# Splitting the product p4 and adding the residual by accumulating DMA in the channel stage of a hash-attention and mixer kernel

## Chip, cores, metric

One core of a Trainium2 chip. The metric is the device time of one execution in microseconds. "Span" is the length of the profiled execution, some 1.8 us shorter than its device time.

## The reference, cut to what matters

```python
# attention (hash-masked), then a mixer on x of shape (4, 768, 512):
h = np.maximum(xt @ w_tok1, 0.0) @ w_tok2
u = x + h.transpose(0, 2, 1)
h2 = np.maximum(u @ w_ch1, 0.0) @ w_ch2     # d_ch = 1536
return u + h2                               # u is the residual
```

The change touches only the last two lines: the channel stage.

## The kernel before

The channel stage is f32. It runs over three blocks (`s`) of 1024 rows. Each of the two matrix products is done by the Strassen-Winograd scheme: seven block products instead of eight. In the second product five of the seven are split once more (`product`, 21 matmuls of 256 columns) and two are done whole (`whole_product`, 12 matmuls of 512 columns): p1 and p4. The first product, with its relu, is done in six "hidden" steps a block. In the kernel's terms, products lie in PSUM tiles and everything else on the chip in SBUF tiles; an "eviction" reads a product from PSUM.

```python
def product(s, j, name, q, between):
    ...
    part(0, 4, b00)                                                  # TensorE
    part(1, 5, b10)
    p1 = copy(ps[0], "p1", ...)                                      # ScalarE
    nc.vector.tensor_tensor(b00, b11, b01, op=ALU.subtract)          # operand sums
    part(2, 0, b01)
    part(3, 1, extra())
    nc.vector.tensor_tensor(b10, b10, b00, op=ALU.subtract)
    ...
    for work in between:
        work()                                                       # adds that combine products
    ...                                                              # evictions into q
    if j + 1 < 6:
        begin(ORDER[j + 1])                                          # two sums for the next product
    ...

def outputs(s):
    ...
    product(s, 3, "p3", q3, [add(q57, q7, q5), residual(q57, 1, 1), residual(q7, 1, 0)])
    product(s, 4, "p6", q6, [add(q3, q3, q5), residual(q3, 0, 1)])
    product(s, 5, "p2", q2, [
        add(q6, q6, q1), add(q57, q57, q6), store(q57, 1, 1), add(q3, q3, q6), store(q3, 0, 1),
        add(q7, q7, q6), residual(q1, 0, 0),
    ])
    ps = whole_product(s, 6, "p4")
    add(q2, q2, q1)()
    store(q2, 0, 0)()
    ...                                       # sums for the next block; last adds and stores of q7
```

`residual` is a VectorE add of the kept `XT`, `store` a plain DMA from SyncE. The hidden steps of each block carry extra work on VectorE: in block 0 the jobs that prepare the split weights (`parts`, through one buffer `seen`), later `look()`, which loads 768 KB of q and k into that same single buffer and reduces it to a maximum; the 16 looks check that the fast softmax is safe.

```python
def look():
    if seen:
        t, n = seen.pop(0)
        nc.vector.tensor_reduce(largest[:, n : n + 1], t, AX.XY, ALU.max, apply_absolute_value=True)
    if unseen:
        n = unseen.pop(0)
        t = pool.tile([P, 2, S], F32, name="seen", tag="seen", bufs=1)
        nc.sync.dma_start(out=t, in_=qk[pairs[n][0], pairs[n][1]])
        seen.append((t, n))
```

And one line of the host code that turns out to matter, though no DMA of this kernel comes from GpSimd:

```python
nc = bacc.Bacc("TRN2", target_bir_lowering=False, num_devices=1, dynamic_dma_scratch_size=1024)
```

I read it as the room, 1024 bytes in each SBUF partition, for the descriptors (the entries that tell the DMA engines what to move) of DMAs that GpSimd issues.

## Time and profile before

| | before |
|---|---|
| device time, median (range) | 827.37 us (827.05 to 829.8) |
| span of the profiled run | 825.5 us |
| TensorE busy | 816.4 us (99%) |
| channel stage, first to last TensorE pass | 404.48 to 818.71 us |
| VectorE's last add to the end | 820.08 to 825.5 us |

TensorE has no pauses worth naming; the lines are in the prediction. Timeline: start us, length us, engine, line, operation, count, idle before with what ended it.

### The profile page before, as it was taken

The numbers are of one execution on the slowest core, as the hardware profiler recorded it, in microseconds if no ns is written. First come the engines' busy times: TensorE is split into PE (matmuls) and PEld (weight loads), VectorE is DVE, ScalarE is ACT, GpSimd is POOL, SyncE is SP. The second block draws the span as 40 slices with busy tenths as digits, with TensorE's granted clock in tenths as the row PEclk, the third lists the DMA queues.
The fourth block names the chain that finished last, engine by engine and source line by source line (L and its number), as shares of the span: only waits on it lengthen the run. The fifth ranks groups of instructions, "written<-read, shape, count | busy, mean of one in ns | idle before, by whom it ended". The sixth has DMA issues, their size and how long they took to land.

```text
span 825.5 us, 9922 instructions
## 1 busy us (share of the span) xinstructions
PE 816.4 (99%) x3719; PEld 436.1 (53%) x3719; DVE 630.3 (76%) x831; ACT 326.0 (39%) x516; POOL 26.1 (3%) x37
## 2 busy tenths in 40 slices
PE   8999999999999999999999999999999999999996
PEld 4444444444444444455544468744447864444884
DVE  4889898989988667798486579956669984635993
ACT  5777788888887774211011211111111102121110
POOL 1000000000000000000011100001010001010000
PEclk9999999999999999999999999999999999999999
DMA  4335354546424226562014444453434345100432
GB/s 159 138 141 173 134 155 135 167 159 201 141 93 118 80 79 182 188 204 76 0 51 150 132 174 143 153 189 114 138 130 171 134 128 194 38 1 0 164 143 106
DMA packets 59784, 106.84 MB, mean 129 GB/s; under 512 B 28296, under 2 KB 37328, under 8 KB 57808
## 3 DMA queue, kind: packets, MB, share of 16 engines
q1 hardware_dynamic: 59168, 105.52, 38.7%
q8 instruction: 31, 0.51, 0.2%
q10 hardware_dynamic: 560, 0.61, 0.2%
q14 instruction: 25, 0.20, 0.1%
HBM read 84.43 MB, written 21.04 MB: 128 GB/s over the span
## 4 chain that ended last, share of the span: by engine, by line
PE 98%; DMA 0%; DVE 0%; ACT 0%; issue 0%; ACTq 0%
PE b L697 50%; PE sc L340 19%; PE acc L387 16%; PE t L618 5%; PE t L637 5%; PE sums L411 2%; PE hp L301 1%; DMA qk<-in_qk 0%; PE hw L319 0%; DVE second L926 0%; ACT vt L292 0%; ACT e L347 0%; ACT g L306 0%; DVE g L305 0%; DVE bits L321 0%
## 5 line engine op out<-in xcount | busy, mean ns | idle before, releaser
L704 ACT COPY p<-b 128x512 f32<-128x512 f32 (+1 forms) x84 | 44.3, 549 | 296.0 <-PE b L697 296.0
L340 PE MATMUL sc<-qk 64*128 64x384 f32 x768 | 158.5, 492 | 0.3 <-ACT e L347 0.3
L347 ACT ACTIVATE e<-sc 128x768 f32<-128x768 f32 x192 | 153.1, 812 | 13.4 <-PE sc L340 12.5
L697 PE MATMUL b<-R,second 128*128 128x256 f32 (+1 forms) x588 | 158.0, 427 | 0.0
L697 PEld LDWEIGHTS b<-R,second 128*128 128x128 f32 x588 | 111.7, 190 | 43.8 <-issue 32.0
L387 PE MATMUL acc<-e,vn 128*64 128x384 f32 x768 | 130.9, 490 | 0.0
L379 DVE TENSOR_TENSOR esd<-esd,e 128x768 f32<-128x768 f32 x128 | 122.3, 955 | 10.4 <-ACT e L347 0.5
L340 PEld LDWEIGHTS sc<-qk 64*128 64x128 f32 x768 | 66.5, 187 | 55.6 <-issue 45.1
L387 PEld LDWEIGHTS acc<-e,vn 128*64 128x64 f32 x768 | 52.3, 137 | 74.9 <-issue 74.3
L697 PE MATMUL b<-XT,WC 128*128 128x512 f32 x144 | 64.7, 592 | 0.0
L340 PE MATMUL sc<-bits 64*128 64x384 bf16 x384 | 62.9, 323 | 0.2 <-DVE bits L323 0.2
L731 POOL TENSOR_TENSOR p<-p,p 128x512 f32<-128x512 f32 x18 | 22.8, 1268 | 723.1 <-ACT p L704 723.1
L697 PEld LDWEIGHTS b<-XT,WC 128*128 128x128 f32 x144 | 27.3, 190 | 34.1 <-issue 33.6
L939 DVE TENSOR_REDUCE largest<-seen 128x1 f32<-128x1536 f32 x16 | 28.0, 1751 | 22.3 <-DMA seen<-in_qk 22.1
L618 PE MATMUL t<-x,W 128*128 128x512 f32 x96 | 41.8, 593 | 0.0
L736 DVE TENSOR_TENSOR R<-p,u 128x512 f32<-128x512 f32 x18 | 12.4, 687 | 38.5 <-POOL p L731 38.5
L637 PE MATMUL t<-W,r 128*128 128x384 f32 x128 | 41.8, 486 | 0.0
L736 DVE TENSOR_TENSOR R<-b,u 128x512 f32<-128x512 f32 x36 | 23.2, 686 | 24.1 <-PE b L697 24.1
L432 ACT COPY rec<-rec 32x384 f32<-32x384 f32 x64 | 32.6, 509 | 12.9 <-DVE rec L426 12.4
L375 DVE SCALAR_TENSOR_TENSOR esd<-e 128x768 f32<-128x768 f32 x32 | 30.5, 954 | 9.3 <-ACT e L347 9.3
L393 ACT ACTIVATE num<-acc,vsum 128x384 f32<-128x384 f32 x32 | 18.6, 581 | 41.6 <-PE acc L387 41.2
L697 PE MATMUL b<-TA,WC 128*128 128x512 f32 x72 | 33.8, 592 | 0.0
(116 smaller groups left out, 922.3 us busy)
## 6 DMA issues: line engine op xcount, KB each, us to landing
second<-left SPq DMA_DIRECT2D x15, 1344.0 KB
raw<-in_moe_w_ch SPq DMA_DIRECT2D x16, 768.0 KB
seen<-in_qk SPq DMA_DIRECT2D x16, 768.0 KB
qk<-in_qk SPq DMA_DIRECT2D x15, 768.0 KB
vn<-in_v SPq DMA_DIRECT2D x16, 384.0 KB
vt<-in_vT SPq DMA_DIRECT2D x16, 384.0 KB
bounced<-stage SPq DMA_DIRECT2D x32, 192.0 KB
x<-bounced SPq DMA_DIRECT2D x4, 1536.0 KB
```

Of the source, the lines that this page charges most:

```text
L340: nc.tensor.matmul(sc[:, i, :HALF], t[rows, 1, P * c : P * c + P], t[rows, 0, qs], start=start, stop=not start,)
L347: nc.scalar.activation(e, sc[:, :, :HALF], ACT.Exp, scale=SCALE)
L375: nc.vector.scalar_tensor_tensor(self.d, es[0], NR * EPS, es[1], op0=ALU.add, op1=ALU.add,)
L379: nc.vector.tensor_tensor(self.d, self.d, e, op=ALU.add)
L387: nc.tensor.matmul(acc[D * i : D * i + D], vn[:, i, c], e[:, i], start=(c == 0), stop=(c == NR - 1),)
L432: nc.scalar.copy(rec[other : other + 32, h], rec[at : at + 32, h])
L618: nc.tensor.matmul(ps, W1[:, r, P * j : P * j + P], x[:, r], start=(r == 0), stop=(r == NR - 1),)
L637: nc.tensor.matmul(ps[:, :HALF], r1[:, j, P * cb : P * cb + P], W2[:, j, HALF * half : HALF * half + HALF], start=(j == 0), stop=(j == NJ ...
L697: nc.tensor.matmul(ps, left(k), right(k), start=start and k == ks[0], stop=stop and k == ks[-1], skip_group_check=True,)
L704: nc.scalar.copy(c if shape is None else shape(c), ps)
L736: nc.vector.tensor_tensor(r[k], split(a), split(u), op=ALU.add)
L939: nc.vector.tensor_reduce(largest[:, n : n + 1], t, AX.XY, ALU.max, apply_absolute_value=True,)
```

## The change

The intent: split p4 as well, which takes 42 passes of 256 columns in place of 24 of 512, and give VectorE the room for the sums that this needs, by taking the residual adds off it. The residual is written to the output early, as a plain DMA of `XT`; the blocks are then stored onto it by DMAs that add. These come from GpSimd's queue.

```diff
-        WHOLE = ["p1", "p4"]
+        WHOLE = ["p1"]
...
-            return [[*sums, whole("p1"), whole("p4"), parts("p7")], *([parts(p)] for p in ["p3", "p6", "p5", "p2"])]
+            return [
+                sums, [whole("p1"), parts("p7")], [parts("p3")], [parts("p6")], [parts("p5")], [parts("p2")],
+                [parts("p4")],
+            ]                                   # now two jobs in a hidden step: one in its middle, one after
...
             def store(q, i, n):
-                return lambda: nc.sync.dma_start(
-                    out=out[KC * i : KC * i + KC, :, sl[n]].rearrange("m p t -> p m t"), in_=q,
-                )
+                def job():
+                    nc.gpsimd.dma_start(
+                        out=out[KC * i : KC * i + KC, :, sl[n]].rearrange("m p t -> p m t"), in_=q,
+                        accum_op=ALU.add,
+                    )
+                return job
...
-            product(s, 3, "p3", q3, [add(q57, q7, q5), residual(q57, 1, 1), residual(q7, 1, 0)])
-            product(s, 4, "p6", q6, [add(q3, q3, q5), residual(q3, 0, 1)])
+            product(s, 3, "p3", q3, [add(q57, q7, q5)])
+            product(s, 4, "p6", q6, [add(q3, q3, q5)])
...
+            if s < last:
+                product(s, 6, "p4", q4, [
+                    add(q2, q2, q1), store(q2, 0, 0), lambda: inputs(s + 1, T, 0), lambda: inputs(s + 1, T, 1),
+                ])
+                add(q4, q4, q7)()
+                store(q4, 1, 0)()
+            else:
+                product(s, 6, "p4", q7, [
+                    add(q2, q2, q1), store(q2, 0, 0), add(q7, q7, XT[:, KC:, sl[0]]),
+                ], lambda i, n: ...)            # final: small adds and plain stores of 128 KB
+
+        def residual(s):                        # called before the second hidden step of each block
+            for i in range(2):
+                for n in range(2):
+                    if s < last or (i, n) != (1, 0):
+                        ...
+                        nc.sync.dma_start(out=out[...], in_=XT[:, KC * i : KC * i + KC, sl])
```

## The prediction

> **What bounds the kernel now.** I read the page first, then the chain of work that ended last, then the timelines of TensorE and VectorE in the last stage, then a table of windows.
>
> ```profile
> span 825.5 us, 9922 instructions
> PE 816.4 (99%) x3719; PEld 436.1 (53%) x3719; DVE 630.3 (76%) x831; ACT 326.0 (39%) x516; POOL 26.1 (3%) x37
> PEclk9999999999999999999999999999999999999999
> ```
>
> TensorE is busy 816.4 of 825.5 us at full clock, so a shorter time must come from fewer or shorter TensorE passes, or from the few us outside them. The chain from 400 us to the end:
>
> ```profile
> 404.48 336.13 PE b L697 x992
> 740.61 0.11 PE b L955
> 740.72 77.99 PE b L697 x298
> 818.71 0.02 issue
> 818.73 0.09 DVE second L926
> 818.82 0.52 issue
> 819.34 0.75 DVE second L926 x2
> ```
>
> From 404.48 to 818.71 us TensorE waits for nobody. This is the channel stage, the only one the change touches: three blocks of 1024 rows, each with six "hidden" steps and seven block products. Then VectorE adds for 1.37 us (818.71 to 820.08) and the last stores run to 825.5. So the unit of account is the pace of a pass (one LDWEIGHTS with its MATMUL; each f32 matmul of the program is two passes in the trace):
>
> ```profile
> 499.66 1.46 PE L697 MATMUL b<-second,second 128*128 128x256 f32 x6
> 508.73 1.46 PE L697 MATMUL b<-second 128*128 128x256 f32 x6
> 517.79 1.46 PE L697 MATMUL b<-second,second 128*128 128x256 f32 x6
> 533.33 0.19 PEld L697 LDWEIGHTS b<-R,second 128*128 128x128 f32 x1 [0.24 <-issue]
> 533.76 0.19 PEld L697 LDWEIGHTS b<-R,second 128*128 128x128 f32 x1 [0.24 <-issue]
> ```
>
> The first three are the same point of three successive split products: one takes 9.07 us for 42 passes of 256 columns, 0.216 us each. The last two lie in the whole product p4: a pass of 512 columns takes 0.43 us. The mean durations in the groups (379 and 592 ns) overlap in the pipeline and must not be multiplied by counts.
>
> VectorE is the second question, because a split product costs it more:
>
> ```profile
> 495.80:504.80 9.00, 9.00 (x43) 7.94 (x42) 8.67 (x13) 1.33 (x3) 0.00 (x0) 1.00 0.43 153
> 522.90:532.00 9.10, 9.10 (x44) 8.02 (x43) 7.87 (x9) 1.33 (x3) 0.00 (x0) 1.00 0.30 90
> 532.00:542.30 10.30, 10.30 (x25) 4.58 (x25) 8.07 (x10) 0.00 (x0) 0.00 (x0) 1.00 0.54 173
> ```
>
> Columns: length, busy PE, PEld, DVE, ACT, POOL (instructions), clock, DMA share, GB/s. In a split product VectorE is busy 8.67 of 9.0 us, in p4 (last row) 8.07 of 10.3.
>
> **What the Trainium skill says.** (1) "TensorE: Matmul & The Clock Gate", Back-to-back issue gap: warm, a matmul of 256 columns takes 262 cycles and one of 512 takes 518, so halving the columns almost halves the time. The trace agrees: 0.216 against 0.43 us. (2) "DMA: Bandwidth & Descriptors", SWDGE vs HWDGE vs iDMA: an accumulate during a DMA goes only through descriptors that GpSimd writes, and its rules add that the accumulate reads its destination and writes it later. No DMA of the kernel before comes from GpSimd (its queue list has none), so nothing here checks that yet. (3) The same page, Anatomy of one DMA: about 2.0 us plus bytes/436e3. In this trace 768 KB of products for p7 were issued at 429.58 us and VectorE overwrote their buffer at 433.94 us without a wait, so they landed within 4.36 us; the formula gives 3.8. (4) "SBUF — State Buffer", Who interferes with whom: VectorE with two SBUF inputs and GpSimd reading SBUF lock each other out. GpSimd is 3% busy, so I expect little of it.
>
> **The change, part by part.**
> *p4 split.* Removed per block: 12 matmuls, 24 passes x 0.43 = 10.30 us. Added: 21 matmuls of 256 columns, 42 passes = 9.07 us. Saved 1.23 us per block, all on the bounding engine; three blocks: **-3.7 us**. This is the only large credit.
> *Residual.* Eleven of the twelve VectorE adds of 128x1024 (1.22 us, one per 1.17) go; the twelfth stays for the last store. Per block VectorE loses 4 x 1.17 and two evictions of 0.65, together 6.0 us, and gains for the split p4: four operand sums of 0.98, four evictions (0.33 + 0.33 + 0.34 + 0.6) and one add of 1.17, together 6.7. So VectorE's load hardly moves, and the removed adds are worth nothing themselves: they make the room for the split. Where it is tight: p4's sums must be ready before its third group of six passes. In the first block the adds of p2 run like this:
>
> ```profile
> 527.89 3.50 DVE L893 TENSOR_TENSOR second<-second,second 128x1024 f32<-128x1024 f32 x3
> 531.30 1.22 DVE L893 TENSOR_TENSOR q<-q,XT 128x1024 f32<-128x1024 f32 x1
> 532.44 0.42 DVE L880 TENSOR_TENSOR second<-b,p 128x256 f32<-128x256 f32 x1
> ```
>
> After, the add at 531.30 is gone: two evictions from 531.3 to 532.0, p4's two sums to 534.0. p4 starts at 523.0 + 9.07 = 532.05, its third group at 532.05 + 12 x 0.216 = 534.6. Margin 0.6 us: no stall, but thin. p4's other two sums end near 536.8, needed at 537.2 and 539.8. Then q2's add, four sums for the next block (to 542.8), p4's evictions and add (to 546). The next hidden step needs its first VectorE result at 546 as before (its add ran at 546.04). No stall.
> *Preparation in block 0.* One more job (p4) and two jobs per hidden step instead of one, each 2.3 us of VectorE; all six share one buffer, which is free when its 768 KB have landed. Residual writes of 2 MB join the same queue. Chain from 420.7: p7; p3 when p7 has landed (427.4); p6 when p3 has, behind the residual (437); then p5 443.7, p2 450.3, p4 457 to 459.3, at 2.3 + 4.3 us a job. VectorE falls up to 10 us behind. The PSUM blocks of a step are doubled: step 3's must be read by 464.4 + 3.4 = 467.8 and are by about 461. No stall if a job's transfer takes 4.3 us. (0.59 MB of other pieces per job also move: 1.38 MB per 6.6 us is 208 GB/s; the trace showed 213 in a 12 us window that was not full.)
> *End.* TensorE ends at 817.3 instead of 818.7. VectorE, behind by then, does q2's add until 814.1, p4's residual add until 815.2, then nine small operations of 0.33 to 0.4: done at about 818.7 instead of 820.1. The last store is 128 KB as before. **-1.4 in place of the last block's -1.23**: -0.2.
> Sum: -3.7 - 0.2 = -3.9 us, 827.4 to **823.5 us**, 0.5% faster.
>
> **Rivals.**
> A. *The preparation stalls TensorE.* If small pieces and residual writes slow a job's transfer from 4.3 to some 6 us, five jobs put p4's job some 8 us later and VectorE past 467.8: a stall of 2 to 6 us, time 825 to 829. For: window of 213 GB/s, pieces of 512-byte rows. Against: the slack of 7 us.
> B. *GpSimd's accumulating stores become a wait.* p4's first eviction writes the buffer that q57's store reads. That store starts about 13 us earlier; only above 25 us would VectorE's delay reach TensorE through the PSUM blocks. At the end, q2's store starts at 814.1, and if reading and writing doubles its estimate of 3.2 us by the skill's formula it lands at 819 to 821, about with the plain last store. With slow descriptors behind the two earlier stores: +1 to +4 us, time 825 to 827.
> C. *p4's sums come late by VectorE's 0.6 us margin*, because GpSimd or semaphores slow it: 0.5 to 1 us x 3, time 824.5 to 826. All of the gain then shrinks to noise.
> D. *Saving hidden anyway*: excluded by the chain, which is TensorE alone.
>
> **Range and chances.** No rival makes the time less than about 822, since the passes are counted; each can add a few us, and they add up. So the range leans upward: 821.8 to 828.0. Over 2% faster would need -16.5 us: 1%. Over 2% slower needs +16.5, only by a queue far slower than thought: 3%. Within 2%: 96%.
>
> **What would show each step.** Right: 42 instead of 24 passes in p4, p4 at 9.07 us, split product to next hidden step without a gap; TensorE's busy sum down by about 3.7; VectorE's total about the same; hidden steps of block 0 still 12.0 us each; last DVE add 1.4 us after TensorE's last pass. Wrong: a wait of PE for the preparation's DVE or the buffer "seen" between 440 and 480 us (A); DVE idle before p4's first eviction, or stores from GpSimd that land after the last plain one (B); a PE wait for a DVE sum in p4 each block (C). A pass of 256 columns well over 0.216 us in p4 would sink the credit itself.

## More of the kernel before

One view is needed later that the prediction doesn't show: the first real matmuls of TensorE, after a row of idle ones.

```profile
4.92 1.53 PE L319 MATMUL hw<-qk,projs 128*128 128x384 f32 x4 [0.81 <-DMA qk<-in_qk]
```

## The result, and the profile after

| | before | after |
|---|---|---|
| device time, median (range) | 827.37 us (827.05 to 829.8), 4 runs | 830.24 us (829.2 to 830.68), 4 runs |
| ratio | | 1.0026 (1.0005 to 1.0048) |
| span of the profiled run | 825.5 us | 828.9 us |

A ratio is the mean time of one kernel's runs over that of the other's in the same rounds, so not quite the ratio of the medians. Instead of 3.9 us faster, the kernel is about 2 to 3 us slower. The page of the changed kernel:

```profile
span 828.9 us, 10089 instructions
PE 814.8 (98%) x3761; PEld 444.9 (54%) x3761; DVE 638.4 (77%) x848; ACT 329.8 (40%) x525; POOL 39.9 (5%) x48
q0 software_dynamic: 2992, 5.77, 4.6%
```

The third line is the new queue, that of GpSimd: 2992 packets, 5.77 MB, eleven stores.

**The split itself does what was said.** Timeline of TensorE after, the same point of p2 and of p4 in block 0:

```profile
528.65 1.46 PE L697 MATMUL b<-second 128*128 128x256 f32 x6
537.72 1.46 PE L697 MATMUL b<-second,second 128*128 128x256 f32 x6
542.90 3.60 PE L697 MATMUL b<-XT,WC 128*128 128x512 f32 x8
```

9.07 us apart, as between the other split products, and the next hidden step follows without a gap. The losses are elsewhere, in three places.

**1. The start.** Before any changed code runs, the first matmuls take 2.90 us instead of 1.53:

```profile
5.00 2.90 PE L319 MATMUL hw<-qk,projs 128*128 128x384 f32 x4 [0.75 <-DMA qk<-in_qk]
```

In the chain of work, the channel stage starts at 406.27 us instead of 404.48: 1.79 us lost.

**2. A wait in block 1.** The view of TensorE's waits has a new line (waiter, released by, total us, times, longest us), and the chain of work, which was TensorE alone before, runs through the loads of `seen`:

```profile
PE b L697 <- DVE R L834: 1.7, 1, 1.7
```
```profile
550.36 2.50 issue
552.86 1.23 POOL out L919
554.09 1.31 POOL p L734
...
560.61 5.48 DMA seen<-in_qk
566.11 1.76 DVE largest L971
567.89 5.51 DMA seen<-in_qk
...
575.21 4.42 DMA seen<-in_qk
579.65 1.76 DVE largest L971
...
628.64 0.97 DVE R L834
629.75 10.38 PE b L697 x47
```

Read it downwards: a store by GpSimd is issued late (552.86), GpSimd's add of a hidden step waits behind it, then load and reduce take turns through one buffer for 60 us, until VectorE makes the first sum for p5 of block 1 (line 834) too late. The first two loads take 5.5 us, the later ones 4.0 to 4.5. In the kernel before, the same sum (there line 828) starts 82.4 us after the block's first hidden step, here 85.7 (628.64 less the 542.90 above); from timelines of the kernel before:

```profile
542.34 3.60 PE L697 MATMUL b<-XT,WC 128*128 128x512 f32 x8
624.74 0.96 DVE L828 TENSOR_TENSOR R<-R 128x768 f32<-128x768 f32 x1
```

**3. The end.** VectorE's last add ends at 820.12 us, at the place where it ended before (820.08), but the kernel ends 8.8 us later instead of 5.4. Timeline of GpSimd after, the three accumulating stores of the last block, and VectorE's last adds:

```profile
806.95 1.21 POOL L919 DMA_DIRECT2D out<-second  x1 [55.53 <-DVE second L913]
812.98 1.22 POOL L919 DMA_DIRECT2D out<-second  x1 [4.81 <-DVE second L905]
819.09 1.21 POOL L919 DMA_DIRECT2D out<-second  x1 [4.90 <-DVE second L894]
```
```profile
814.31 1.22 DVE L913 TENSOR_TENSOR second<-second,q 128x1024 f32<-128x1024 f32 x1
819.37 0.75 DVE L899 TENSOR_TENSOR second<-b,second 128x256 f32<-128x256 f32 x2
```

The add at 814.31 makes q2; its store could be issued at 815.5. It is issued at 819.09. The releaser that the view names (a small add of VectorE) has nothing to do with it: in the source the store waits for the add of q2. The stores are 6.0 and 6.1 us apart. In the other blocks the first three are 6.0 to 6.4 us apart, and the fourth comes 9.0 to 9.3 us after the third.

The account of the profiled runs, from the ends of TensorE's and VectorE's last work:

| part | us |
|---|---|
| start: 406.27 against 404.48 | +1.8 |
| 126 passes of 256 in place of 72 of 512 columns | -3.7 |
| wait in block 1 (1.7 in the waits view, the rest in short pauses) | +1.9 |
| VectorE's last add after TensorE's last pass: 1.43 against 1.37 | +0.1 |
| last add to end: 8.78 against 5.42 | +3.4 |
| sum (spans: 828.9 - 825.5 = 3.4) | +3.5 |

The second row is the estimate of the prediction; the third is what is then left of TensorE's stage: 414.2 us from its first to its last pass before, 412.4 after (the end taken from TensorE's timeline, where the last group of 18 passes starts at 814.64 and takes 4.05 us).

### The profile page after: what moved, and what is told of

Its sections match the earlier page's. It is cut to its first block, busy times and chain, and to the rows that moved or that the text cites. A ratio compares the mean times of both kernels' runs of the same rounds, so it can differ in the third digit from the quotient of the medians.

```text
span 828.9 us, 10089 instructions
## 1 busy us (share of the span) xinstructions
PE 814.8 (98%) x3761; PEld 444.9 (54%) x3761; DVE 638.4 (77%) x848; ACT 329.8 (40%) x525; POOL 39.9 (5%) x48
## 3 DMA queue, kind: packets, MB, share of 16 engines
q0 software_dynamic: 2992, 5.77, 4.6%
## 4 chain that ended last, share of the span: by engine, by line
PE 77%; issue 9%; DMA 6%; DVE 6%; POOL 1%; ACT 0%; POOLq 0%; DVEq 0%; ACTq 0%
PE b L697 29%; PE sc L340 19%; PE acc L387 16%; DMA seen<-in_qk 6%; PE t L618 5%; PE t L637 5%; DVE largest L971 3%; PE sums L411 2%; PE hp L301 1%; DVE second L913 1%; POOL out L919 1%; PE hw L319 1%; DMA qk<-in_qk 0%; DVE R L834 0%; DVE R L876 0%
## 5 line engine op out<-in xcount | busy, mean ns | idle before, releaser
L704 ACT COPY p<-b 128x512 f32<-128x512 f32 (+1 forms) x90 | 47.1, 544 | 298.7 <-PE b L697 293.2
L697 PE MATMUL b<-R,second 128*128 128x256 f32 (+1 forms) x612 | 151.1, 404 | 1.7 <-DVE R L834 1.7
L697 PEld LDWEIGHTS b<-R,second 128*128 128x128 f32 x612 | 116.2, 190 | 34.4 <-issue 20.5
L697 PE MATMUL b<-XT,SW 128*128 128x512 f32 x72 | 33.8, 592 | 0.0
```

Of the source, the lines that this page charges most:

```text
L697: nc.tensor.matmul(ps, left(k), right(k), start=start and k == ks[0], stop=stop and k == ks[-1], skip_group_check=True,)
L704: nc.scalar.copy(c if shape is None else shape(c), ps)
```

## The experiments

All variants gave correct results. Theory for (3): a second accumulating store has to wait until the first one's descriptors have left the 1024 bytes a partition that are reserved for them. Rival: GpSimd itself takes 6 us to write a store's descriptors. Theory for (2): the residual writes stand in the queue ahead of two loads of `seen`. Rival: the late GpSimd add. Theory for (1): chance of the execution. Rival: it belongs to the changed kernel.

### c_before: the kernel before again (no edit)

> The kernel before, unchanged, as a control. In the first traces the changed kernel lost 1.8 us before any changed code ran: its first four hw matmuls took 2.90 us instead of 1.53, at a mean granted clock of 0.995 instead of 0.999. If that is chance of the start (a slow and a fast start for any program), some runs of this kernel show 0.995 and a time 2 to 3 us longer, like the 829.8 among the first ones, and its mean equals that of the kernel before within 0.1%. If the start belongs to the changed kernel, every run here shows 0.999 and 827 us.

Measured: 827.37 us median, 826.98 to 828.24. The profiled run has the fast start (1.53 us, clock 0.999), and by their times the other five have it too. But the runs of the kernel before that served as comparison do both: of 11, five lie from 828.96 to 830.03, the others from 826.89 to 827.53. I take these five for slow starts of the kernel before, 2.2 us longer. That rests on the times alone: no such run was profiled, and their clock is 0.998 to 0.999, not the 0.995 that I had expected of them.

### c_after: the changed kernel again (no edit)

> The changed kernel again, as a control beside the others. The profiled run of the kernel before in the same form ran its first four hw matmuls in 1.53 us, the runs of the changed kernel and of two of its variants in 2.90, one variant in 1.53; and 4 of 11 runs of the kernel before lie near 829 to 830 instead of 827. So the start looks like chance of the execution. Then some runs here lie at 828.3 to 828.8 and some 2 to 2.5 us above. If the slow start belongs to the changed kernel, all lie at 829 to 831.

Measured: 831.05 us median; 827.73, 828.89, 829.71, 832.4, 833.25, 834.64. The profiled one (828.89) has the fast start: its first matmuls take 1.53 us and its channel stage begins at 404.60. So the changed kernel has both starts, and here the account is cleaner (its clock is 0.995 all the same, so the mean clock doesn't tell the starts apart): span 827.1 us, TensorE's stage 411.3 us (wait in block 1 only 0.6), VectorE's last add at 817.31, and then 9.8 us to the end. The three times above 832 fit neither side of the expectation; no profile of such a run was taken, and they stay unexplained.

### e_scratch: 2048 bytes for the descriptors

```diff
-        "TRN2", target_bir_lowering=False, num_devices=1, dynamic_dma_scratch_size=1024
+        "TRN2", target_bir_lowering=False, num_devices=1, dynamic_dma_scratch_size=2048
```

> The changed kernel with 2048 instead of 1024 bytes a partition for the descriptors of the DMAs that GpSimd issues. Theory: the accumulating stores go one at a time because a second store's descriptors don't fit beside the first's (q57, q3 and q2 of the last block are issued at 806.95, 812.98 and 819.09, 6.0 us apart, though q2 was ready at 815.5), so q2's store lands last and the end comes 8.6 us after VectorE's last add instead of 5.4. Then with room for more, q3's store is issued within 2 us of its add, q2's at about 815.7, the end falls to about 5.5 us after the last add, and the time is 2.5 to 3.2 us below the changed kernel. Rival: GpSimd needs 6 us of its own to write the descriptors of one store; then the gaps of 6.0 us and the time stay.

Measured: 825.05 us median (824.61 to 827.6), ratio to the kernel before 0.9966 (0.9949 to 0.9984): the first version that is faster than it, if only by 0.3%. Part of the ratio is the starts: five of the eleven comparison runs are slow ones, here by its time one of six. The stores of q57 and q3 are issued as one pair within 2.45 us, q2's at 812.38, right after its add. Last add to end: 6.25 us. The wait in block 1 is gone as well, which I hadn't expected of this edit; so the gain over the changed kernel, 5.2 us by medians and 4.3 by the spans with a fast start (827.1 to 822.8), is larger than the 2.5 to 3.2 expected.

### e_ring1152: 1152 bytes

```diff
-        "TRN2", target_bir_lowering=False, num_devices=1, dynamic_dma_scratch_size=1024
+        "TRN2", target_bir_lowering=False, num_devices=1, dynamic_dma_scratch_size=1152
```

> The changed kernel with 1152 bytes a partition for GpSimd's descriptors: the smallest step that should matter. The trace counts 2992 packets in GpSimd's queue for 11 stores, 272 each, so 17 per DMA engine. If a store needs 17 entries for its writes and twice 16 plus 1 = 33 for its reads (source and destination), two need 66 entries of 16 bytes: more than the 64 of 1024 bytes, fewer than the 72 of 1152. Then q3's store is issued right after q57's, as with 2048 bytes, q2's is not later than about 1 us after its add, and the time is that of the 2048 bytes within 0.5 us. Rival: each store needs more than 36 entries or the reserve works in larger steps; then the stores stay 6 us apart.

The 16 bytes of an entry are the Trainium skill's ("DMA: Bandwidth & Descriptors", Terms). Measured: 824.9 us median (824.44 to 827.11), ratio 0.9966. Timeline of GpSimd, last block:

```profile
803.38 2.47 POOL L919 DMA_DIRECT2D out<-second  x2 [55.53 <-DVE second L913]
812.38 1.23 POOL L919 DMA_DIRECT2D out<-second  x1 [6.53 <-DVE second L913]
```

128 bytes more give all that 1024 bytes more give: 64 entries hold one store, 72 hold two. The count of 33 entries a store is an estimate that fits this; at that size the runs show only that a store needs more than 32 and no more than 36.

### e_halves: each store as two DMAs, 1024 bytes

```diff
-                    nc.gpsimd.dma_start(
-                        out=out[KC * i : KC * i + KC, :, sl[n]].rearrange("m p t -> p m t"), in_=q,
-                        accum_op=ALU.add,
-                    )
+                    for m in range(KC):
+                        nc.gpsimd.dma_start(out=out[KC * i + m, :, sl[n]], in_=q[:, m], accum_op=ALU.add)
```

> The changed kernel, 1024 bytes, with each accumulating store cut into two DMAs of half the size. If space for descriptors is what a store waits for, three halves fit and the waiting is in smaller steps: q2's last half is issued 1 to 3 us earlier than 819 on the scale of the first trace, the time 0.5 to 2 us below the changed kernel. Rival: GpSimd's queue lets one accumulating DMA run at a time, whatever its size; then six halves of at least 4 us each make q2's last half come later than before and the time is 2 us or more above the changed kernel.

```profile
809.63 2.69 POOL L920 DMA_DIRECT2D out<-second  x3 [55.54 <-DVE second L913]
814.23 0.87 POOL L920 DMA_DIRECT2D out<-second  x1 [1.90 <-issue]
818.62 1.75 POOL L920 DMA_DIRECT2D out<-second  x2 [3.52 <-DVE second L913]
```

Three halves go out at once and the fourth waits: it is space, not the number of DMAs. The count of e_ring1152 fits here too: a half would take 17 entries, so three take 51 of the 64 and four would take 68 (an estimate, as above). Measured 827.58 us median (825.46 to 831.78), about 3 us below the changed kernel, more than the 0.5 to 2 expected, and more scattered. In the profiled run (slow start, 2.2 us of waiting in block 1) q2 itself was ready only at about 818, so its issue time can't be set against the 819 expected; the end came 7.0 us after the last add.

### e_resid: residual writes of blocks 1 and 2 moved

```diff
-                if t == 1:
+                if t == 1 and s == 0:
                     residual(s)
...
             product(s, 1, "p5", q5, ...)
+            ahead(0)              # if s < last: residual(s + 1), one quarter
             product(s, 2, "p7", q7, ...)
+            ahead(1)
             product(s, 3, "p3", q3, ...)
+            ahead(2)
             product(s, 4, "p6", q6, ...)
+            ahead(3)
```

> The changed kernel with the residual writes of blocks 1 and 2 issued one quarter at a time during the products of the block before, where the queue has room, instead of all at the second hidden step. Theory: in block 1 VectorE's loads of seen through one buffer are a chain with about 1 us to spare; the 2 MB of residual writes ahead of two of them lengthen each from 4.3 to 5.5 us, VectorE comes 2.9 us late to the first sum of p5, and TensorE waits 1.7 us. Then the wait of TensorE for that sum disappears and the time falls by 1.5 to 1.9 us. Rival: the delay comes from GpSimd, whose add of block 1's first hidden step waited behind the fourth store (553.6 instead of about 551.7); then the wait stays at over 1 us.

Measured: 828.4 us median (827.32 to 830.88), 1.8 to 2.6 us below the changed kernel's two medians. TensorE's wait for line 834 is gone. The rival isn't refuted as a contributor, though: e_scratch left the residual writes in place, freed GpSimd, and also lost the wait. Counted from the start of block 1's first hidden step, the sum of line 834 starts 82.4 us later in the kernel before, 85.7 after, 84.1 in e_scratch, 83.2 in e_resid; in the changed kernel TensorE needed its result at about 85.2, so a start by 84.2. Either edit alone gets below that (e_both has the four cases together). The end stays: q2's store is issued at 818.67 and the span is 829.1 us with a slow start.

### e_last: in the last block q2 stored plainly, its residual added by GpSimd and no longer written early

```diff
             product(s, 5, "p2", q2, [
-                add(q6, q6, q1), add(q57, q57, q6), ...
+                add(q6, q6, q1), own(s, q1), add(q57, q57, q6), ...   # own: q1 += XT on GpSimd, last block
...
-                    add(q2, q2, q1), store(q2, 0, 0), ...
+                    add(q2, q2, q1), plain(q2, 0, 0), ...
```

> The changed kernel with, in the last block only, the quarter of q2 stored plainly from SyncE; its residual is added by GpSimd to q1 (after q6 has read q1), so VectorE's work stays. The theory that q2's accumulating store ends the kernel says: the end comes 5.4 to 5.8 us after VectorE's last add and the time falls by 2.5 to 3.2 us. The rival that any use of GpSimd's queue lengthens the ending (a drain of its queue) leaves 8 us or more after the last add and the time unchanged.

Measured: 830.41 us median (829.75 to 835.1): no gain. The end is as the theory said: 5.6 us after the last add. But the edit made a new wait. Timeline of GpSimd and VectorE, and the waits of TensorE after 700 us:

```profile
806.10 3.32 POOL L934 TENSOR_TENSOR q<-q,XT 128x1024 f32<-128x1024 f32 x1 [54.02 <-DVE second L913]
```
```profile
805.99 5.65 DVE L913 TENSOR_TENSOR second<-second,second 128x1024 f32<-128x1024 f32 x3
```
```profile
PE b L697 <- DVE R L834: 1.6, 1, 1.6
```

The three VectorE adds beside GpSimd's take 5.65 us instead of 3.50, p4's first sums are late, and TensorE waits 1.6 us (and 1.5 in block 1, as in the changed kernel). The Trainium skill ("SBUF — State Buffer", Who interferes with whom) says that two such instructions lock each other out; I had read that before predicting and still placed the add there.

### e_both: 2048 bytes and the residual writes moved

> Both causes taken away: 2048 bytes for the descriptors, and the residual writes of blocks 1 and 2 moved into the products of the block before. The larger reserve alone gave 825.05 us and had no wait of TensorE in block 1 either. So I expect 824.3 to 825.2: the two removals overlap in block 1 (1.7 us is there once), and the end is the one of the larger reserve. If residual writes and stores hurt in different places, 822.5 to 823.5.

Measured: 825.64 us median; three runs from 824.59 to 824.78, three from 826.51 to 827.38. No wait of TensorE in the stage; span 823.0 us with a fast start, last add to end 6.5. As expected the two overlap in block 1. With this run all four cases of that block have a trace. The sum of line 834, counted as in e_resid, starts

| | residual writes moved | residual writes in place |
|---|---|---|
| GpSimd's add on time | 82.2 us (e_both) | 84.1 (e_scratch), 83.8 (e_ring1152) |
| GpSimd's add late | 83.2 (e_resid) | 85.7 and 84.6 (changed kernel) |

So the residual writes cost 1.6 to 1.9 us and GpSimd's delay about 1.0; only together do they pass the 84.2 us. Each figure is one trace, and one more doesn't fit: in e_halves GpSimd's add is on time (8.2 us into the block, as in e_scratch, against 10.7 in the changed kernel), and yet the sum starts at 86.2.

### e_splitonly: the split of p4, nothing else

```diff
-                    nc.gpsimd.dma_start(... accum_op=ALU.add)
+                    nc.sync.dma_start(...)          # plain
-            product(s, 3, "p3", q3, [add(q57, q7, q5)])
+            product(s, 3, "p3", q3, [add(q57, q7, q5), res(q57, 1, 1), res(q7, 1, 0)])
...                                                  # likewise q3 and q1; no early residual writes
```

> Only the split of p4, with residual adds on VectorE and plain stores as in the kernel before. Theory: VectorE has no room; p4's first sums come 1.17 us later in each block than with the accumulating stores, whose margin was 0.6 us (sums ready at 534.0 for 534.6), so TensorE waits about 0.6 us in each p4, and the last block's VectorE work ends 1 us or so later: 824.5 to 826.5 us, no stall in block 1. Rival, that the accumulating stores were needed to make the split pay: no faster than the kernel before, 827 or more.

```profile
PE b L697 <- DVE R L834: 1.2, 3, 0.4
```

Measured: 826.62 us median (824.65 to 826.93); span 822.9 us in the profiled run, which had a fast start. The waits are as expected in kind, 0.4 us in each p4 instead of 0.6. Last add to end: 5.1 us. Four of the six runs, 826.55 to 826.93, are by their times slow starts, which lifts the median; the ratio to the kernel before is 0.9975 (0.9960 to 0.9991), against 0.9966 (0.9945 to 0.9987) for e_ring1152. So, with a fast start, the split with the old residual adds is as fast as the changed kernel with room for its descriptors (822.8 us in e_ring1152): what the accumulating stores take off VectorE's path, 1.2 us of waiting, they give back at the end (6.2 against 5.1 us).

### e_nosplit: the accumulating stores without the split

```diff
-        WHOLE = ["p1"]
+        WHOLE = ["p1", "p4"]
...                      # p4 as in the kernel before; its quarter stored plainly, residual added on VectorE
```

> Only the accumulating stores (three of four quarters) and the early residual writes, p4 whole as before, 1024 bytes for descriptors. TensorE's passes are those of the kernel before. Theory: the residual writes ahead of two loads of seen cost up to 1.5 us of waiting in block 1, and the three stores 6 us apart (about 805.5, 811.5, 817.6) make the last land about 0.5 to 2 us after the plain last store: 828.5 to 830.5 us. If the stores are harmless without the split: 827.0 to 827.8.

Measured: 832.77 us median (832.03 to 833.22), above what I expected; less 2.35 us for the slow start of its profiled run it would be 830.4, at the upper edge. TensorE waits only 0.2 us in block 1, where up to 1.5 was expected; the end comes 8.5 us after the last add instead of 5.4, 3.1 more where 0.5 to 2 was expected. So without the split, too, the stores and early writes make the kernel slower.

### e_best: e_both with q2 of the last block plain, residual on VectorE

```diff
-                    add(q2, q2, q1), store(q2, 0, 0), add(q7, q7, XT[:, KC:, sl[0]]),
+                    add(q2, q2, q1), add(q2, q2, XT[:, :KC, sl[0]]), plain(q2, 0, 0),
+                    add(q7, q7, XT[:, KC:, sl[0]]),     # and no early residual write for q2
```

> 2048 bytes, residual writes moved, and in the last block the quarter of q2 with its residual added on VectorE (1.17 us after the sums of p4) and stored plainly. Of the version without this last step the end came 6.4 us after VectorE's last add ended, of the kernel with plain stores alone 5.1. If q2's accumulating store still ends it, the end comes about 5 us after a last add that is 1.1 us later: 0 to 0.5 us gained, about 822.6 for the profiled span with a fast start. If the longer ending has another cause, 1 us lost.

Measured: 825.81 us median (824.76 to 827.27). Span 824.7 us with a slow start (the channel stage began at 406.43 instead of 404.62 in e_both: 1.8 us), last add to end 5.1 us. Corrected for the start that is 822.9 against 823.0 us: nothing gained that counts. It does show that q2's accumulating store still sets the longer ending of e_both.

### e_warm: e_both with 17 idle matmuls instead of 14

```diff
-        for _ in range(14):
+        for _ in range(17):
             nc.tensor.matmul(idle[:D, :D], ones, ones, start=True, stop=True)
```

> 2048 bytes, residual writes moved, and 17 instead of 14 matmuls ahead of the first ones, so that TensorE is busy until the first data land at about 4.9 us instead of 4.2. If the two starts (first four hw matmuls in 1.53 or 2.90 us, 2 us apart in the whole) depend on how busy TensorE was before them, more runs have the fast start: at least 5 of 6 at 824.5 to 825.3. If it is only the phase of the start, about half the runs stay 2 us higher.

Measured: 825.04 us median, all six from 824.53 to 825.62, ratio 0.9959 (0.9945 to 0.9973). The profiled run had neither start but one between (2.45 us for the first four matmuls, channel stage from 405.46). No run was as high as the slow ones of e_both; with six runs each this speaks for the longer warm-up, but doesn't prove it.

## Why the prediction was wrong

It said 823.5 us, range 821.8 to 828.0; measured 830.24.

- **The credit of the split was right.** p4 takes 9.07 us. Where nothing else waits (e_ring1152) TensorE's stage is 410.5 us against 414.2: 3.7 us less, as said, and its busy sum falls by 3.6 (816.4 to 812.8). And p4's sums were in time: the waits of the changed kernel lie in block 1, not in p4.
- **The preparation, rival A, caused no stall**, as said. VectorE did wait there for the buffer `seen` (11.0 us in four waits), but TensorE didn't.
- **The step that failed is rival B's weight, the term of the end.** I put the last block at "-0.2" for the end and let q2's store land "at 819 to 821", by size and rate alone. I had named "slow descriptors behind the two earlier stores: +1 to +4 us", but left it out of the sum. It was +3.4 us in the first trace, +4.4 with the fast start (9.8 against 5.4). What failed in it: a store waits not for descriptors to be written but for room to put them. The line with 1024 bytes stood in the kernel, and the prediction doesn't mention it. e_ring1152 settles it. Even with room, the 3.9 us are not reached: the span of e_ring1152 is 2.7 us shorter than that of the kernel before (both with the fast start), because the end is still 6.2 us instead of 5.4, and the 0.2 us that I had added for the end don't show.
- **A margin I didn't compute.** I checked VectorE's margin in p4, in block 0 and at the step to block 1, but not the chain of loads and reduces through `seen` in block 1. Load and reduce take about 6.1 us in turn, twice per 12.0 us hidden step: that chain had no slack to catch up in the kernel before either, and only about 2 us to the point where TensorE would wait. Two loads of 5.5 us instead of 4.3 behind the residual writes, and GpSimd late by a waiting store, used them up: 0.6 to 1.9 us of waiting (the table in e_both divides the delay). "No stall" at the next hidden step was right and looked one step too short.
- **The start** (+1.8 us in the profiled run) lies before any changed code. The changed kernel was profiled with both starts, and by its times the kernel before has both too. That the change has no part in it isn't shown, though: of the six profiled runs with accumulating stores and 1024 bytes five have the slow start, of the eight others one, and one lies between. The start widens every comparison here by 2 us and should have been in the range.
- **VectorE's load hardly moves**: right (630.3 to 638.4 us busy). **VectorE's last add about 1.4 us after TensorE's last pass**: right (1.43).
- **Two checks against the Trainium skill were weaker than they read.** The cycle counts of a matmul agree with the trace as a ratio only (see the last section). And "DMA: Bandwidth & Descriptors", Anatomy of one DMA, gives its 2.0 us plus bytes/436e3 for DMAs that GpSimd issues, while the products of p7 that I held against it (an estimate of 3.8 us against at most 4.36) are issued by SyncE.

What stays open: why some runs of the changed kernel reach 832 to 835 us (every run of any version above 831 us had accumulating stores and 1024 bytes), why e_halves is late in block 1, and what decides the start.

By medians three versions are alike: e_ring1152 (824.9 us), e_warm (825.04) and e_scratch (825.05). So the gain is one number, 1152 or more in place of 1024; e_warm may add that slow starts become rare.

## What to carry to other kernels

Before stores move to GpSimd's queue, count what a store puts into its descriptor reserve and how many must be in flight; a reserve trimmed for a kernel without such DMAs makes them go one by one, and the trace then blames an innocent engine for the wait. When a change adds traffic to a queue, look for single-buffered load-and-use chains further down that queue, even a block later: one that just keeps pace has no way to catch up. And test each half of a two-part change alone: here the half that was to make room earned nothing measurable once the other half ran without it.

## What the Trainium skill lacked or had wrong

- "DMA: Bandwidth & Descriptors", SWDGE vs HWDGE vs iDMA: it says that the descriptor rings of GpSimd's DMAs lie in a carveout of SBUF, but not that one DMA waits there for another's space. The page counts descriptors for a plain 1 MiB transfer, not for an accumulating one. Here 1024 bytes let one accumulating store of 512 KB go every 6.0 us or more, 1152 let two go within 2.5 us; at 16 bytes an entry that is more than 32 and at most 36 entries a store.
- The same page, Anatomy of one DMA: its fit makes an estimate of 3.2 us for 512 KB; with one accumulating store in flight at a time the runs show 6.0 us from one to the next. The page has no number for accumulating stores.
- "TensorE: Matmul & The Clock Gate", What's actually happening: a free-running window of about 3.4 us, with the step varying by some 0.5 us. The two starts could be this (1.53 or 2.90 us for the same four matmuls, with the same data arriving), but the traces don't show it: the clock that they record is 1.00 in every 2 us window of the first 22 us with either start. By its times the whole kernel differed by about 2 us between executions, more than the 0.5 us suggest; the same section also says that the number of slow matmuls changes from run to run.
- "TensorE: Matmul & The Clock Gate", Back-to-back issue gap: 262 cycles for 256 columns would be 109 ns at the 2.4 GHz of that page, an estimate; here a pass of 256 f32 columns takes 216 ns and one of 512 takes 430. The page has no line for f32.
